# A block-sparse attention with a gated feed-forward behind it: fused scores, wider turns, six chunks for the dense rows, and another plan

## The chip, the cores and the metric

One Trainium2 chip; the kernel is one launch on one of its cores. The time is device time in microseconds (us), as the median of several runs. A core has five engines with queues of their own: TensorE (PE, matmuls, results into eight PSUM banks), VectorE (DVE), ScalarE (ACT), GpSimd (POOL) and SyncE (SP, which here issues DMA transfers). 16 DMA engines move the data.

## The reference

Four batches, eight heads, 768 tokens in 24 blocks of 32, head size 64. Each query block sees its own block and its neighbours, the first and the last block, and three sampled blocks; the first and the last query block see everything. The attention's output goes through a gated feed-forward (512 to 1536 to 512).

```python
scores = np.matmul(q, k.transpose(0, 1, 3, 2)) / np.sqrt(D)
mask = np.abs(blk_i - blk_j) <= 1
mask = mask | (blk_i == 0) | (blk_j == 0) | (blk_i == n_blocks - 1) | (blk_j == n_blocks - 1)
for qb in range(n_blocks):
    for kb in sampled_blocks[qb]:
        mask[qb*32:(qb+1)*32, kb*32:(kb+1)*32] = True
attn = softmax(np.where(mask, scores, -1e9))
x = np.matmul(attn, v)            # (4, 8, 768, 64) -> (3072, 512)
out = (sigmoid(x @ w_gate) * (x @ w_val)) @ w_out
```

## The kernel before, in words

The function builds a list of operations first. Each one has an engine (or a choice of two), a planned duration, the operations it depends on, a priority, and the buffers it takes and releases. A planner (`Planner.run`) then simulates the engines and picks, again and again, the operation that can start first, the lower priority number among those that can start at nearly the same time. The order that comes out is written into the queues of the engines and fixed. A wait at run time therefore holds up everything behind it on the same engine. `switch` is the planned price of a change of PE between full-size matmuls and matmuls on 64x64 or 64x32 tiles of the array; transfers are planned with one rate for SP and one for POOL.

**Load (L375, POOL's queue).** For each batch K, V and Q are loaded with a cast to 16 bits into four staging buffers `stg` of 96 partitions, eight tokens per partition. In batch 0 the order is K, V, Q. The weights (L390, L398) follow in chunks, which the list `GATES` holds back until certain gathers have been issued.

**Turn (L484, L492, L497, L499).** K and Q are transposed on PE, per pair of heads in 16 transposes of 96x64 (two heads side by side, as 64-column tiles of the array), and evacuated by DVE or ACT into `KT` and `QT`. Tokens in `KT` stand in the order (j, p): token 8p+j lies at column 96j+p.

**V's road (L526, L534, L546, L563, L569, L627).** DVE regroups V by rows; four transfers write it to the DRAM buffer `scr`; from there SP gathers, for each query block, the three neighbours (L563, several blocks at once, into `V1`) and the three sampled blocks (L627, three transfers of 32 KB, into `V2`). The block numbers stand in registers of SP (L413). POOL copies the first and the last block into the remaining 32 rows (L569).

**A step** is two query blocks with all eight heads; a batch has 11. POOL copies the sampled keys into one of four buffers `KG` (L605, three copies per block, and L614 for the first and last block). PE computes masks and scores as 64x32 tiles (L648, L655) into two PSUM banks. DVE takes the maximum in each bank (L666), ACT the exponentials with their sums (L677), DVE the reciprocal (L684) and the scaling (L696; the planner may put it on ACT in its plan, but the instruction written is DVE's). PE transposes the probabilities (L708), DVE or ACT evacuates them (L714), PE multiplies with V (L733), and the result goes to `XA` (L749, L754).

**Dense rows.** For the first and the last query block, per pair of heads: scores over 768 keys in two banks (L774), two maxima and their combination (L784, L785), two exponentials (L792), sum, reciprocal and scaling (L801 to L803), eight transposes of 96 columns (L813), evacuation (L818), eight products (L831), result to `XA` (L848). There are 4 such pieces per batch.

**Feed-forward.** Nine groups of 128, 128, 256, 256, 256, 512, 512, 512 and 512 tokens. For each of 12 chunks of the hidden size: gate and value matmuls (L884, four each), tanh on ACT (L892), product on DVE (L897); then 12 matmuls per 128 tokens (L915), scaling (L922, L924), store (L929). Its evacuations have the first priority in the plan.

**PSUM banks.** Scores use banks 0 to 2 (two for each step), transposes and products 2 and 3, the feed-forward 4 to 7 (the last two groups all eight).

Of the kernel before, what the change touches and what calls it, by code (L numbers as in the profile page):

```python
# [26 lines left out]
NEG = -1.0e30  # L27

# [19 lines left out]

class Planner:
# [10 lines left out]
    def __init__(self):  # L60
        self.ops = []
        self.held = {}

# [5 lines left out]
    def run(self, switch=0.12, dma_lat=1.8):  # L69
        free = {e: 0.0 for e in self.ENG}  # L70
        slot_free = {}
        slot_held = {}
        handles = {}
        dma_free = {e: 0.0 for e in self.ENG}
        lanes = {e: [0.0] * self.LANES for e in self.ENG}
        mode = 128
        for o in self.ops:
            o.outs = []
            o.nwait = len(o.deps) + len(o.after)
            o.ready = []  # L80
# [11 lines left out]
        n = len(self.ops)  # L92
        while len(order) < n:
            best = None
            for e in self.ENG:
                ests = []
                for o in cand[e]:
                    t = free[e]
                    for tr, er, lat in o.ready:
                        t = max(t, tr + (lat if er != e else 0.0))  # L100
                    if o.dma:
                        t = max(t, lanes[e][min(o.ndma, 3) - 1])
                    ok = True
                    got = {}
                    for h, slots in o.acq:
                        c = [(slot_free.get(s, 0.0), k, s) for k, s in enumerate(slots)
                             if s not in slot_held and s not in got.values()]
                        if not c:
                            ok = False
                            break  # L110
                        now = [x for x in c if x[0] <= t]
                        x = min(now, key=lambda x: x[1]) if now else min(c)
                        got[h] = x[2]
                        t = max(t, x[0])
                    if ok:
                        if e == "PE" and o.mode != mode:
                            t += switch
                        ests.append((t, o, got))
                if not ests:
                    continue  # L120
                lo = min(x[0] for x in ests)
                pick = min((x for x in ests if x[0] <= lo + (0.12 if e == "PE" else 0.02)),
# [20 lines left out]
            o.eng, o.dur = e, o.durs[o.engs.index(e)]  # L143
            if e == "PE":
# [6 lines left out]
            if o.dma:  # L151

                share = 3.0 if e == "SP" and dma_free["POOL"] > o.end else 1.0
                dma_free[e] = max(dma_free[e], o.end) + o.dma * share
                if e == "SP":
                    dma_free["POOL"] += o.dma
                o.end = dma_free[e] + dma_lat
                lanes[e] = lanes[e][o.ndma :] + [o.end] * o.ndma
# [4 lines left out]
            for h in o.rel:  # L163
# [3 lines left out]
                slot_free[s] = o.end + o.lat  # L167
            for x in o.engs:
                cand[x].remove(o)
            for w, whole in o.outs:  # L170
                w.nwait -= 1
                w.ready.append((o.end, e, o.lat) if whole else (o.start + o.dur, e, 0.0))
# [9 lines left out]
def kernel(  # L182
# [45 lines left out]
    banks = [psum.tile([128, 512], f32, tag=f"bank{i}", name=f"bank{i}") for i in range(8)]  # L228
# [14 lines left out]

    KT = [sb(f"KT{r}", [128, NP, S]) for r in range(2)]
    QT = [sb(f"QT{r}", [128, NP, S]) for r in range(2)]
    KT4 = [t.rearrange("d a (j p) -> d a j p", p=TP) for t in KT]

    KW4 = [t.bitcast(f32).rearrange("d a (j p) -> d a j p", p=TP // 2) for t in KT]
    stg = [sb(f"stg{r}", [TP, H * TJ * D]) for r in range(4)]
    stages = [("stg", r) for r in range(4)]  # L250
    by_head = lambda t: t.rearrange("p (h j d) -> p h j d", h=H, j=TJ)
    by_row = lambda t: t.rearrange("p (j h d) -> p j h d", h=H, j=TJ)
# [14 lines left out]
    DP = [sb(f"DP{s}", [128, TJ, 128]) for s in range(2)]  # L267
    DPT = [sb(f"DPT{s}", [128, TJ, 128]) for s in range(2)]
# [41 lines left out]
    GATES = {7: 2, 9: 4, 10: 6, 11: 8}  # L310
    WCH, WOH = 4, 3

    TURN_DMA = 4
    VGATHER = [("SP", 1.6)] * 4

    K_DMA, KQ_SP = 4, 3.0
    SC_DUR = 0.36
# [14 lines left out]
    def f_memset(o):  # L332
        pin(nc.gpsimd.memset(ones, 1.0))
        pin(nc.gpsimd.memset(mrow, 0.0))
        for d in DP:
            pin(nc.gpsimd.memset(d.rearrange("q j p -> q (j p)").bitcast(f32), 0.0))

    def f_mask(o):
# [5 lines left out]
        pin(V.tensor_scalar(kidx[:, 0 : NB * 3], in0=sbv.rearrange("p a o -> p (a o)"), scalar1=2, scalar2=None, op0=ALU.mult))  # L344
# [16 lines left out]
    o_ms = P("memset", "POOL", 1.4, f_memset, prio=-40)  # L361
# [5 lines left out]
    def load(name, src, b, prio, after=(), parts=1):  # L367
# [4 lines left out]
        for x in range(parts):  # L372
            def f(o, x=x):
                t = by_head(stg[pl.handles[h][1]])[:, x * n : x * n + n]
                pin(nc.gpsimd.dma_start(t, src[b, x * n : x * n + n].rearrange("h (p j) d -> p h j d", j=TJ)))  # L375

            res.append(P(f"ld{name}{b}{x}", "POOL", 0.8, f, after=list(after) + res[-1:], prio=prio,
                         acq=[(h, stages)] if x == 0 else [], dma=3.9 / parts))
# [28 lines left out]
    def f_regs(eng, key, part):  # L407
        def f(o):
            e = {"SP": nc.sync, "POOL": nc.gpsimd}[eng]
            et = {"SP": mybir.EngineType.SP, "POOL": mybir.EngineType.Pool}[eng]  # L410
            src, unit = (kidx, 2) if eng == "POOL" else (vidx, BLK)
# [26 lines left out]
    pgb = bk(4, 5, 6, 7)  # L438
    spool = bk(0, 1, 2)
    early = bk(0, 1, 4, 5, 6)  # L440
    ptpool = bk(2, 3)
    xpool = bk(3, 2)
# [13 lines left out]
    def attention(b, prio0, ldeps):  # L456
# [5 lines left out]
        if b == 0:  # L462
            ldk, hk = load("k", k, b, pp - 0.050, ldeps, np_)
            ldv, hv = load("v", v, b, pp - 0.049, ldk[-1:])
            ldq, hq = load("q", q, b, pp - 0.048, ldv[-1:], np_)
# [8 lines left out]
        for nm, ld, hs, res, TT in (("k", ldk, hk, kops, KT[r]), ("q", ldq, hq, qops, QT[r])):  # L474
            if nm == "q" or b < K_DMA:
                for p in range(NP):
                    h = f"tr{nm}{b}{p}"

                    def f_tr(o, hs=hs, p=p, h=h):
                        t = by_head(stg[pl.handles[hs][1]])  # L480
                        ps = banks[o.slots[h][1]].bitcast(f16)[:, 0:S].rearrange("d (j p) -> d j p", p=TP)
                        for j in range(TJ):
                            for hh in range(2):
                                pin(nc.tensor.transpose(ps[64 * hh : 64 * hh + 64, j, :], t[:, 2 * p + hh, j, :], ident[0:TP, 0:TP]))  # L484

                    tr = P(f"tr{nm}{b}{p}", "PE", 0.47, f_tr, deps=[ld[p * np_ // NP], c_dma] + kq_users[b - 2], prio=pp - 0.040,
                           acq=[(h, early if b == 0 else xpool)], mode=64, rel=[hs] if p == NP - 1 else [])

                    def f_ev(o, nm=nm, p=p, h=h, TT=TT):
                        ps = banks[o.slots[h][1]].bitcast(f16)[:, 0:S]  # L490
                        if nm == "k":
                            pin(copy(o)(TT[:, p, :], ps))  # L492
                            return
                        ps = ps.rearrange("d (j b c) -> d b j c", b=NB, c=4)
                        dst = TT[:, p, :].rearrange("d (b j c) -> d b j c", b=NB, c=4)
# [5 lines left out]
                    res.append(P(f"ev{nm}{b}{p}", ("DVE", "ACT"), (0.48, 0.7), f_ev, deps=[tr], prio=pp - 0.040, rel=[h]))  # L501
            else:

                hsh = f"sh{nm}{b}"

                def f_sh(o, hs=hs, hsh=hsh):
                    t = by_head(stg[pl.handles[hs][1]])
                    d = stg[o.slots[hsh][1]].rearrange("p (a j e d) -> p a j e d", a=NP, j=TJ, e=2)
                    for hh in range(2):
                        pin(nc.vector.tensor_copy(d[:, :, :, hh, :], t[:, hh : H : 2]))  # L510

                shs.append(P(f"sh{nm}{b}", "DVE", 1.3, f_sh, deps=ld, prio=pp - 0.045, rel=[hs], acq=[(hsh, stages)]))

                ldq[0].after.append(shs[0])

                def f_tt(o, hsh=hsh, TT=TT):
                    pin(nc.sync.dma_start(TT.rearrange("d a (j p) -> d (a j) p", p=TP), stg[o.slots[hsh][1]], transpose=True))

                res.append(P(f"tt{nm}{b}", "SP", KQ_SP, f_tt, deps=shs[-1:] + kq_users[b - 2], prio=pp - 0.040, rel=[hsh], dma=3.5))
# [4 lines left out]
        def f_vsh(o):  # L524
            t = by_head(stg[pl.handles[hv][1]])
            pin(nc.vector.tensor_copy(by_row(stg[o.slots[f"vr{b}"][1]]), t.rearrange("p h j d -> p j h d")))  # L526

        vs = P(f"vsh{b}", "DVE", 1.14, f_vsh, deps=ldv, prio=pp - 0.045, rel=[hv],
               acq=[(f"vr{b}", stages)])

        def f_scr(o):
            dst = scr[b].rearrange("(b j c) n -> c b j n", j=TJ, c=4)
            for c in range(4):
                pin(nc.sync.dma_start(dst[c], vrows(o).rearrange("(b c) (j n) -> c b j n", c=4, j=TJ)[c]))  # L534

        sc = P(f"scr{b}", "SP", 3.2, f_scr, deps=[vs], prio=pp - 0.045, dma=2.2, ndma=3)
        scr_ops.append(sc)
        if b == 0:
            FF["gate"][0].after.append(sc)
# [5 lines left out]
        def f_fl(o):  # L545
            pin(nc.sync.dma_start(FL[96:128, 0, :], scr[b][0:BLK, :]))  # L546
            pin(nc.sync.dma_start(FL[96:128, 1, :], scr[b][S - BLK : S, :]))

        fl = P(f"vfl{b}", "SP", 1.0, f_fl, deps=[sc] + fl_users[b - 1], prio=bp - 1.55, dma=0.2, ndma=2)
# [6 lines left out]
        for (i0, n), x in zip(wins, turn):  # L556
# [3 lines left out]
            def f_w(o, i0=i0, n=n, x=x):  # L560
                src = scr[b][(i0 - 1) * BLK : (i0 - 1) * BLK + 96, :]
                src = bass.AP(tensor=src.tensor, offset=src.offset, ap=[[DM, 96], [BLK * DM, n], [1, DM]])
                pin(nc.sync.dma_start(V1[x][0:96, 0:n, :], src))  # L563
# [411 lines left out]
```

## Time and profile before

| | us |
|---|---|
| median of 3 runs (lowest to highest) | 355.77 (355.77 to 358.47) |
| the profiled execution | 354.82 |
| its span, first to last instruction | 353.0 |
| busy in the span: PE, DVE, ACT, POOL | 315.2, 245.2, 211.3, 107.7 |
| last product of the attention (L733) starts | 294.5 |
| DMA: bytes moved, share of 16 engines (SP's and POOL's queue) | 42.05 MB, 27.1% and 25.8% |

Matmuls are pipelined and their ends are modelled, so PE's busy time is an upper bound of the work in it. Lines of groups read: line, engine, operation, output<-input, count, busy us, mean ns, idle time before and who ended it. Lines of the chain and of the timeline begin with the start and the duration in us.

### The profile page before, as it was taken

Reading aid. Unit: us, or ns where it says so; the run is one execution under the profiler, and the core shown is the slowest. Engines: PE = TensorE matmul, PEld = TensorE weight load, DVE = VectorE, ACT = ScalarE, POOL = GpSimd, SP = SyncE. Lnnn points to the kernel's source line nnn. Section 1 sums busy time; section 2 is a strip of 40 time slices with the busy share of each in tenths; the row PEclk is TensorE's granted clock in tenths of the full one; section 3 lists DMA queues with packets and bytes.
Section 4 is the critical chain, followed back from the end, with each engine's and each line's share of the span. In section 5 each row is a group of like instructions: output and inputs, shape, how many; then the busy total and the mean of one; then the engine's idle time right before and its main releaser. Section 6 shows DMA issues by size and latency. Waiting matters only on the chain.

```text
span 353.0 us, 13181 instructions
## 1 busy us (share of the span) xinstructions
PE 315.2 (89%) x4864; PEld 202.8 (57%) x4864; DVE 245.2 (69%) x647; ACT 211.3 (60%) x688; POOL 107.7 (31%) x361
## 2 busy tenths in 40 slices
PE   2557988999797979989999999999999999999995
PEld 1336776667573667667856655555555555444442
DVE  1586889788698785789977999597789594303320
ACT  2265677675494776688866868657765574223321
POOL 5449853016248141354501246331021200000000
PEclk9999989999899998999999999999999999999999
DMA  7996999999943879232343243334313210020002
GB/s 121 195 188 149 190 223 231 223 209 234 231 118 111 167 137 196 79 101 77 113 142 104 83 110 99 116 109 113 84 45 95 87 45 0 2 83 36 3 30 89
DMA packets 44132, 42.05 MB, mean 119 GB/s; under 512 B 5923, under 2 KB 40996, under 8 KB 44068
## 3 DMA queue, kind: packets, MB, share of 16 engines
q1 hardware_dynamic: 28820, 27.06, 27.1%
q0 software_dynamic: 15248, 14.16, 25.8%
q8 instruction: 38, 0.62, 0.7%
q14 instruction: 26, 0.21, 0.2%
HBM read 45.91 MB, written 9.44 MB: 157 GB/s over the span
## 4 chain that ended last, share of the span: by engine, by line
PE 57%; DMA 16%; DVE 11%; ACT 7%; SPq 4%; issue 3%; POOL 0%; ACTq 0%; DVEq 0%; POOLq 0%
PE bank L884 27%; PE bank L915 14%; DMA V<-scr 11%; PE bank L733 4%; ACT P L677 4%; PE bank L708 4%; DVE P L696 3%; DMA stg<-in_v_dram 3%; DVE NM L666 2%; DMA out_dram<-YS 2%; PE bank L655 2%; SPq L627 2%; DVE HT L897 2%; PE bank L648 1%; PE bank L813 1%
## 5 line engine op out<-in xcount | busy, mean ns | idle before, releaser
L677 ACT ACTIVATE P<-bank,NM 128x256 f16<-128x256 f32 x176 | 81.6, 476 | 26.0 <-DVE NM L666 24.8
L605 POOL COPY KG<-KT 128x64 f32 x264 | 51.3, 243 | 112.1 <-PE bank L655 104.4
L884 PE MATMUL bank<-XA,wv 128*128 128x512 f16 (+2 forms) x432 | 82.4, 315 | 1.0 <-DMA wv<-in_moe_w_val_dram 0.6
L884 PE MATMUL bank<-XA,wg 128*128 128x512 f16 (+2 forms) x432 | 82.5, 315 | 0.9 <-ACT TH L892 0.4
L897 DVE SCALAR_TENSOR_TENSOR HT<-TH,bank 128x512 f16<-128x512 f32 (+2 forms) x108 | 54.3, 505 | 39.0 <-PE bank L884 36.6
L892 ACT ACTIVATE TH<-bank 128x512 f32<-128x512 f32 (+2 forms) x108 | 48.9, 458 | 37.7 <-PE bank L884 32.7
L915 PE MATMUL bank<-wo,HT 128*128 128x512 f16 x288 | 65.2, 379 | 2.6 <-DVE HT L897 2.6
L666 DVE TENSOR_REDUCE NM<-bank 128x2 f32<-128x512 f32 x88 | 57.4, 682 | 5.9 <-PE bank L655 5.7
L884 PEld LDWEIGHTS <-wv 128*128 128x128 f16 x432 | 38.8, 101 | 25.4 <-issue 2.2
L884 PEld LDWEIGHTS <-wg 128*128 128x128 f16 x432 | 37.2, 101 | 21.7 <-issue 2.6
L915 PEld LDWEIGHTS <-HT 128*128 128x128 f16 x288 | 27.2, 98 | 34.6 <-issue 3.9
L696 DVE TENSOR_SCALAR P<-P,ZZ 128x256 f16<-128x256 f16 x176 | 45.8, 320 | 1.5
L569 POOL COPY V<-FL 32x1024 f32<-32x1024 f32 (+1 forms) x32 | 30.1, 978 | 23.7 <-PE bank L733 16.8
L733 PE MATMUL bank<-PTS,V 128*128 128x64 f16 x704 | 30.7, 196 | 6.5 <-DMA V<-scr 6.1
L677 ACT ACTIVATION_READ_ACCUMULATOR P<-bank,NM 128x1 f32 x176 | 36.4, 207 | 0.0
L733 PEld LDWEIGHTS <-V 128*128 128x128 f16 x704 | 27.6, 100 | 14.3 <-issue 4.6
L708 PE MATMUL bank<-ident,P 128*128 128x128 f16 x352 | 29.1, 227 | 5.4 <-ACT DP L792 1.2
L749 ACT CAST XA<-bank 64x256 f16<-64x256 f32 x62 | 22.6, 364 | 15.3 <-PE bank L733 13.2
L708 PEld LDWEIGHTS <-P 128*128 128x128 f16 x352 | 23.5, 102 | 11.0 <-issue 5.6
L714 DVE COPY PTS<-bank 128x1024 f16<-128x1024 f16 x37 | 25.3, 683 | 5.7 <-PE bank L708 5.0
L484 PE MATMUL bank<-ident,stg 96*64 96x96 f16 x512 | 18.3, 228 | 11.9 <-DMA stg<-in_k_dram 6.1
L924 ACT ACTIVATE YS<-bank 128x512 f32<-128x512 f32 x22 | 13.1, 598 | 24.1 <-PE bank L915 21.1
(61 smaller groups left out, 307.0 us busy)
## 6 DMA issues: line engine op xcount, KB each, us to landing
V<-scr SPq DMA_DIRECT2D x264, 32.0 KB
out_dram<-YS SPq DMA_DIRECT2D x24, 256.0 KB
V<-scr SPq DMA_DIRECT2D x16, 288.0 KB
stg<-in_v_dram POOLq DMA_DIRECT2D x4, 768.0 KB, 10.2
scr<-stg SPq DMA_DIRECT2D x16, 192.0 KB
V<-scr SPq DMA_DIRECT2D x8, 384.0 KB
stg<-in_k_dram POOLq DMA_DIRECT2D x3, 768.0 KB, 12.4
stg<-in_q_dram POOLq DMA_DIRECT2D x3, 768.0 KB, 13.1
```

The lines of the kernel that those rows point to most:

```text
L569: pin(nc.gpsimd.tensor_copy(vt[x][96:128, 0:n, :].bitcast(f32), FL[96:128, c : c + 1, :].bitcast(f32).broadcast_to([BLK, n, DM // 2])))
L605: pin(nc.gpsimd.tensor_copy(t[:, :, 1 + n], KW4[r][:, :, :, bass.ds(vals[(i % 8) * 3 + n], 2)]))
L666: pin(nc.vector.tensor_reduce(NM[pl.handles[hz][1]][:, 2 * hh : 2 * hh + 2], t, axis=AX.X, op=ALU.max, negate=True))
L677: pin(nc.scalar.activation(pb[:, u, :], t[:, u, :], AF.Exp, bias=NM[z][:, x : x + 1], scale=1.0, accum_out=ZZ[z][:, x : x + 1]))
L696: pin(nc.vector.tensor_scalar(pb[:, u, :], in0=pb[:, u, :], scalar1=ZZ[z][:, 2 * hh + u : 2 * hh + u + 1], scalar2=None, op0=ALU.mult))
L708: pin(nc.tensor.transpose(t[:, c * 128 : c * 128 + 128], pb[:, c * 128 : c * 128 + 128], ident))
L714: pin(copy(o)(PTS[pl.handles[hTS][1]].rearrange("k c q -> k (c q)"), banks[o.slots[hT][1]].bitcast(f16)))
L733: pin(nc.tensor.matmul(t[:, u, p, :], vt[:, ws, p * 128 : p * 128 + 128], pt[:, u, c, :, 32 * p : 32 * p + 32], start=(c == 0), stop=(c == ...
L884: pin(nc.tensor.matmul(t, wt[:, c, f_ * 128 : f_ * 128 + 128], XT[g][:, c, :], start=(c == 0), stop=(c == 3)))
L892: pin(nc.scalar.activation(TH[o.slots[ht][1]][:, 0:n], banks[o.slots[hg][1]][:, 0:n], AF.Tanh, bias=0.0, scale=0.5))
L897: pin(nc.vector.scalar_tensor_tensor(HT[:, f_, hoff : hoff + n], in0=TH[o.slots[ht][1]][:, 0:n], scalar=1.0, in1=banks[o.slots[hv][1]][:, ...
L915: pin(nc.tensor.matmul(t, HT[:, f_, hoff + tt * 128 : hoff + tt * 128 + 128], wo[:, f_, :], start=(f_ == 0), stop=(f_ == NF - 1)))
```

## The change

It has these parts:

1. **Planner.** Transfers of both queues are simulated together (`Transfers`), with lower rates while both queues have work; the price of a mode change is 0.16 instead of 0.12; PE waits up to 1 us (`WAIT`) before it leaves full-size matmuls for a lone small-tile operation; a table `OFFSETS` shifts the priority of each kind of operation in each batch; in planned gaps of PE between 7 and 60 us, dummy matmuls on the identity are put in (`fill`).
2. **Banks.** Pairs of banks are one tile. Scores take pair (0,1) or (2,3), transposes and products bank 4 or 3, the feed-forward banks 5 to 7 (the last two groups all eight).
3. **Fused scores.** In batches 2 and 3 the scores of steps 0 and 1, 2 and 3, and so on, and of the dense pieces 0 and 1, 2 and 3, are one operation of PE. One DVE instruction takes the maxima of both banks of a step.
4. **Head pairs.** In batches 1 to 3, POOL or DVE regroups K and Q by rows first; PE then transposes the 128 columns of a head pair at once, 8 transposes of full width per piece instead of 16. `KT` now holds the tokens in order.
5. **Dense rows.** 6 chunks of 128 keys instead of 8 of 96; one maximum and one exponential instruction over both banks.
6. **V.** It is loaded first in batch 0, as 128 partitions of six tokens, and written to `scr` by one transfer; in batch 0 SP or ACT may issue that transfer, the first window and the two edge blocks. Q of batch 0 is loaded and turned in two parts by tokens (64 and 32 of the 96 partitions). There are five staging buffers.
7. **Order of loads.** Weights wait for gathers of blocks 4, 7, 9, 10 and 11; the loads of the next batch wait for the gather of block 12 (batch 0) or 10.
8. **Scaling.** Where the planner picks ACT for L696's work, ACT now does it. The copies of edge blocks may go to DVE.

```diff
-    def run(self, switch=0.12, dma_lat=1.8):
+    def run(self, switch=0.16):
...
+                if e == "PE" and mode == 128:
+                    full = [x for x in ests if x[1].mode == 128]
+                    part = [x for x in ests if x[1].mode != 128 and x[0] <= free[e] + switch + 0.05]
+                    if full and min(x[0] for x in full) <= free[e] + 0.05 and len(part) == 1 and free[e] < self.since.setdefault(id(part[0][1]), free[e]) + WAIT:
+                        ests = full
...
+    twin = [psum.tile([128, 1024], f32, tag=f"bank{i}", name=f"bank{i}") for i in range(4)]
+    banks = [twin[i // 2][:, 512 * (i % 2) : 512 * (i % 2) + 512] for i in range(8)]
...
-    GATES = {7: 2, 9: 4, 10: 6, 11: 8}
+    GATES = {0: 4, 2: 7, 4: 9, 6: 10, 8: 11}
+    LGATE = {1: 12, 2: 10, 3: 10}
+    PAIRS = ["d0 d1", "d2 d3", "s0 s1", "s2 s3", "s4 s5", "s6 s7", "s8 s9"]
+    TOGETHER = [[], [], PAIRS, PAIRS]
...
-    pgb = bk(4, 5, 6, 7)
-    spool = bk(0, 1, 2)
-    early = bk(0, 1, 4, 5, 6)
-    ptpool = bk(2, 3)
-    xpool = bk(3, 2)
+    pgb = bk(5, 6, 7)
+    spool = [tuple(bk(x, x + 1)) for x in (0, 2)]
+    spool0 = [tuple(bk(x, x + 1)) for x in (0, 2, 6)]
+    early = bk(0, 1, 2, 5, 6)
+    ptpool = bk(4, 3)
+    xpool = bk(4, 3)
+
+    def scores(b, unit, name, dur, fn, deps, prio, acq, rel=()):
+        both = next((x for x in TOGETHER[b] if unit in x.split()), unit)
+        if (b, both) not in made:
+            fns = [fn]
+            def f(o):
+                for x in fns:
+                    x(o)
+            made[b, both] = P(name, "PE", dur, f, deps=deps, prio=prio, mode=32, acq=acq, rel=rel), fns
+            return made[b, both][0]
+        o, fns = made[b, both]
+        fns.append(fn)
+        o.deps += deps
+        o.acq += acq
+        o.rel += rel
+        o.durs = (o.durs[0] + dur,)
+        return o
...
-            ldk, hk = load("k", k, b, pp - 0.050, ldeps, np_)
-            ldv, hv = load("v", v, b, pp - 0.049, ldk[-1:])
-            ldq, hq = load("q", q, b, pp - 0.048, ldv[-1:], np_)
+            ldv, hv = load("v", v, b, pp - 0.050, ldeps)
+            ldk, hk = load("k", k, b, pp - 0.049, ldv[-1:], np_)
+            ldq, hq = load("q", q, b, pp - 0.048, ldk[-1:], np_, tokens=True)
...
+                def f_sh(o, hs=hs, hsh=hsh):
+                    t, d = by_head(stg[pl.handles[hs][1]]), by_row(stg[o.slots[hsh][1]])
+                    if o.eng == "POOL":
+                        pin(nc.gpsimd.tensor_copy(d.bitcast(f32), t.bitcast(f32).rearrange("p h j d -> p j h d")))
+                    else:
+                        pin(nc.vector.tensor_copy(d, t.rearrange("p h j d -> p j h d")))
...
+                                pin(nc.tensor.transpose(ps[:, j, :], t[z, j * DM + p * 128 : j * DM + p * 128 + 128], ident[z, z]))
...
+                            pin(copy(o)(TT[:, p, :].rearrange("d (p j) -> d p j", j=TJ), ps.rearrange("d (j p) -> d p j", j=TJ)))
...
-            for c in range(4):
-                pin(nc.sync.dma_start(dst[c], vrows(o).rearrange("(b c) (j n) -> c b j n", c=4, j=TJ)[c]))
+            pin(queue(o).dma_start(scr[b].rearrange("(p j) n -> p (j n)", j=VJ), vrows(o)[:, 0 : VJ * DM]))
...
+            def f_mx(o, hS=hS, hz=hz):
+                t = twin[pl.handles[hS[0]][1] // 2].rearrange("p (x n) -> p x n", n=256)
+                pin(nc.vector.tensor_reduce(NM[o.slots[hz][1]][:, 0:4], t, axis=AX.X, op=ALU.max, negate=True))
...
+                    if o.eng == "ACT":
+                        for u in range(2):
+                            pin(nc.scalar.activation(pb[:, u, :], pb[:, u, :], AF.Copy, scale=ZZ[z][:, 2 * hh + u : 2 * hh + u + 1]))
+                        return
...
+            def f_dmx(o, h0=h0, hz=hz):
+                pin(nc.vector.tensor_reduce(NM[o.slots[hz][1]][:, 0:1], all_keys(h0), axis=AX.XY, op=ALU.max, negate=True))
...
+                pin(nc.scalar.activation(DP[o.slots[hDP][1]].rearrange("p (x n) -> p x n", x=2), all_keys(h0), AF.Exp,
+                                         bias=NM[z][:, 0:1], scale=1.0, accum_out=ZZ[z][:, 0:1]))
...
+                for j in range(VJ):
+                    pin(nc.tensor.transpose(t[:, j * 128 : j * 128 + 128], DP[o.slots[hDP][1]][:, j : S : VJ], ident))
...
+    def fill(t0, t1, mode, held, freed):
+        t0 = max(t0, 7.0)
+        n = int((t1 - t0 - 0.2) / FILL_DUR)
+        if n < 4 or t0 > FILL_END:
+            return None
...
+            for x in range(n):
+                pin(nc.tensor.matmul(banks[y[1]][:, 0:128], ident, ident, start=True, stop=True, skip_group_check=True))
...
+    for o in pl.ops:
+        o.prio += OFFSETS.get(kind(o), 0.0)
```

## The prediction

> **What bounds the kernel now.** I began with the busy time by stage: us of the stage, then busy us of each engine, the clock that TensorE (PE) was granted and the DMA share.
>
> ```profile
> 0.00:20.00 20.00, 8.40 (x221) 6.80 (x224) 7.99 (x27) 5.52 (x9) 11.37 (x38) 1.00 0.91 160
> 20.00:60.00 40.00, 30.93 (x616) 25.26 (x609) 32.87 (x97) 25.98 (x102) 25.81 (x72) 0.96 1.08 195
> 60.00:180.00 120.00, 108.02 (x2066) 80.25 (x2066) 98.80 (x273) 83.93 (x280) 44.04 (x148) 0.97 0.72 153
> 180.00:300.00 120.00, 119.41 (x1751) 68.82 (x1747) 93.82 (x235) 81.52 (x275) 26.52 (x104) 1.00 0.30 88
> 300.00:353.00 53.00, 48.43 (x224) 21.69 (x222) 11.70 (x17) 14.33 (x24) 0.00 (x0) 0.99 0.10 40
> ```
>
> From 180 us on PE has no gap (119.41 of 120): there, PE work removed is time removed, and relief for the other engines is worth nothing. Before 180 us it has gaps. Second view, the chain of waits over the first 60 us:
>
> ```profile
> 2.76 9.44 DMA stg<-in_v_dram
> 12.32 1.24 DVE stg L526
> ...
> 17.11 3.08 DMA scr<-stg
> ...
> 21.18 8.31 DMA V<-scr
> ...
> 35.65 6.48 DMA V<-scr
> 42.15 5.36 DMA V<-scr
> ```
>
> That is the road of V: loaded third (behind K), regrouped, written to DRAM by four transfers (issued 13.57 to 17.89), gathered back. The gathers set the end of this stage. Third, the costliest groups, for durations:
>
> ```profile
> L666 DVE TENSOR_REDUCE NM<-bank 128x2 f32<-128x512 f32 x88 | 57.4, 682 | 5.9 <-PE bank L655 5.7
> L696 DVE TENSOR_SCALAR P<-P,ZZ 128x256 f16<-128x256 f16 x176 | 45.8, 320 | 1.5
> L784 DVE TENSOR_REDUCE NM<-bank 128x1 f32<-128x384 f32 x32 | 16.2, 548 | 0.1
> L526 DVE COPY stg<-stg 96x4096 f16<-96x4096 f16 x4 | 5.2, 1295 | 1.6 <-DMA stg<-in_v_dram 1.4 <-issue 0.2
> ```
>
> Busy PE is not PE at its pitch, so I counted the matmuls of 60 to 180 us and multiplied by the undisturbed pitches of the timeline: 512 columns 0.216 us (96 in 20.72 at the end of the chain), eight 128-column transposes 0.45, sixteen of L733 0.47, one step's scores 0.50 and 0.10 for entering the 32-row mode. That gives about 98 us, so 22 of the 120 are lost. The waits name one part: L733 on V gathers 4.9 us; and the clock falls to 0.50 for 3.41 us from 92.4 and from 133.4, each just after such a wait, 1.7 us lost each time. DMA is thus behind 8.3; the other 13.7 belong to evacuations on DVE and ScalarE (ACT) and to waits between groups.
>
> **PE work removed.** (a) Dense rows: in 16 pieces, 8 transposes and 8 products become 6 and 6: 64 matmuls at 0.056 = 3.6 us. (b) K and Q of batches 1 to 3: 24 pieces, now 16 half transposes in 0.46 us plus some 0.09 to enter the 64-row mode (four 256-wide matmuls take 0.44, but 0.53 when this piece follows); then 8 full ones, 0.36 to 0.45 by the pitch of L708's, with no mode. Gain 0.09 to 0.19 each; some pieces already follow each other, so I take 0.12, 2.9 us (2.2 to 4.6). (c) Fused scores: 7 of 15 pieces go in batches 2 and 3, 14 mode entries at 0.10 = 1.4 us (0 to 2.8). Sum 7.9 us (5.8 to 11.0), on the path where PE is full; where it has gaps it only counts if the next wait moves too, and that is the next term.
>
> A fused piece waits for the copied keys of four units, the whole ring of four buffers, and for banks 0 to 3. Behind it in PE's queue stand feed-forward matmuls. Refilling the ring takes 12 copies of L605 at 0.243 = 2.9 us on POOL, after the piece that frees it. From 180 to 300 us 18 steps ran, 6.7 us each, so 13 us per pair: covered, at no cost. Without that cover each of 14 pieces would pay up to 2.9.
>
> **DVE and ACT.** The two reduce rows give 134 ns for 128 columns, so one reduce over 1024 takes 1.22 against 2 x 0.682: 0.15 x 44 = 6.4 us less DVE. Dense: 0.95 against 2 x 0.548 + 0.249, and the 0.18 sum goes: 9 us less. ACT's dense exponentials: 2 x (0.58 + 0.20) become one of about 1.09, 7.5 us less. All 176 scalings of L696 run on DVE now, those the planner gave to ACT too; in the new code ACT really runs its share. Against this, six regroupings of K and Q (1.3 us by L526; on POOL twice L569's 0.98 for half the data), K's evacuation with a strided read (0.55 now, at most doubled, 16 times). DVE is relieved by 10 to 30 of its 245 us. None of it counts from 180 us on. Of the 13.7 us above I take a third back, 4.5 (0 to 9). The regrouping delays each load's use by 1.2 to 2; batch 1's loads were issued from 52.1 and first turned at 74.1, so they arrive early; uncovered it would be 3 x 2.
>
> A POOL regrouping holds DVE up, too: L696 averages 0.39 us for the 56 that overlap a POOL copy and 0.29 for the others. At most six times 2 us, kept for the range; I count nothing, because DVE has slack against PE in every stage. The Trainium skill (GPSIMD Engine Reference, section Specifications) says that POOL shares its SBUF interfaces with VectorE and contends with its two-port modes. That speaks against putting these copies on POOL, and this trace agrees (0.39 against 0.29); by it alone the sum would lose up to these 12 us.
>
> **Start.** V is now loaded first. The first half of K landed at 6.1 and the second at 8.4, so V lands near 8 rather than 12.2; one transfer (0.5 issue, 3.1 landing, up to 5 beside K and Q) puts it into DRAM near 13.5 rather than 20.2. K comes as much later, but Q completes the same three loads at 16.5 as before, and first scores stay near 17. So the gathers start 6.7 earlier, and products wait for the probabilities' transposes (24.7). Bytes to move are the same; the queue of gathers and weights starts earlier. I take 5 us (0 to 9). The first weights now wait for a V gather's issue, with POOL's key copies behind them in its queue; today they are issued at 18.02, land 7.4 later and are first used at 37.9, 12 us of cover. V's load becomes 1024 packets instead of 768 (95 ns each over 16 engines by the queue rows: 1.5 us more), its way to DRAM 128 instead of 768 (53 ns each: 2.1 less); they cancel. Issuing some of batch 0's transfers from ACT costs ACT 0.4 us each while it idles.
>
> Weights, loads and gathers are reordered by a model in which gathers crawl while POOL loads run. Of the 8.3 us of DMA waits and slow clock I take 5 (0 to 7).
>
> **Dummy matmuls** fill planned PE gaps up to 60 us. In this trace 32 transposes took 1.49 us up to 17 us and 0.87 at 98.5, and the pitch halves at 41.2: the early PE runs at half rate. Half of 22 us of work could shrink, but PE idles 18 of those 40 us, so I take 1 (from -1, dummies ahead of late work, to 4). The Trainium skill (TensorE: Matmul & The Clock Gate, section What's actually happening) has the clock halved by default and after an idle window of about 3.4 us; the lengths of 3.41 agree, though here waits of 2.3 and 2.6 us were enough. By it, with the fill, all of the early half rate would go, about 4 instead of 1.
>
> **Sum**: 7.9 + 4.5 + 5 + 5 + 1 = 23.4. The profiled execution took 354.82 (span 353.0 and 1.8 around it): 331.4; the median of the runs lies 0.95 above that execution, so **332 us**. Bounds: all lower ends save 4.8, all upper ends 40.
>
> **Rivals.** One: transfers bind the start anyway and the chip does not follow the plan's rates; only PE work goes: 355.8 - 7.9 = 348 (345 to 351). For it: DMA share 1.08 to 1.25 from 40 to 90 us, same bytes. Against: only 0.91 before. Chance 0.17. Two: the plan holds everywhere, three quarters to all of the upper ends: 316 to 324. For it: PE idles 11.6 + 9.1 + 12.0 us before 180. Against: every term would have to come out at its best. 0.12. Three, slower: the feed-forward keeps **three banks instead of four**. A gate bank is held for its matmuls, 0.2 to the release and ACT's tanh, a value bank likewise with DVE's product: at 256 columns 0.44 + 0.2 + 0.38 and 0.44 + 0.2 + 0.41, together 2.07 of the 3 x 0.88 bank-us of a chunk; so each evacuation may be late by 0.28 us, at 512 columns (0.86, 0.60, 0.69) by 0.89. Four banks allowed 0.7 and 1.7. A product queued behind a 1.22 us reduce then stops PE 0.94 us (0.33 at 512). With 36 chunks of 256 columns and 24 of 512 that is at most 42 us; it cancels the gain when more than 56% of them meet it. At 70% it is 29: 361 (359 to 373). Against: evacuations have the planner's first priority, and PE has attention work between chunks. 0.11. Within 1%, a mixture: 0.05. The rest, 0.55, is the forecast (324 to 342).
>
> Faster by over 1% (about what a measurement here can tell from no change): 0.55 + 0.17 + 0.12 = 0.84; same 0.05; slower 0.11. The range 316 to 354 leaves out the slower rival and little else.
>
> **What would show it.** Profile after: transposes and products of the dense rows 96 each; reduce about 1.2 us, 44 times; the first V gather near 14 and first products near 25; PE busy share in 60 to 180 above 0.93 and fewer half-clock windows; attention's last product before 280 instead of 294.6. Wrong if PE waits on HT (L897) or TH (L892) at the feed-forward grow past 10 us, if V waits stay at 6, or if PE has new gaps after 180.

## The result, and the profile after

The changed kernel takes **411.50 us** (median of 4 runs, 409.21 to 413.28), the kernel before 355.77 (4 runs, 355.37 to 358.47). The ratio is 1.154 (1.146 to 1.163): 56 us slower, where 332 us were forecast. The profiled execution has a span of 411.5 us.

The same table by stage as before the change: us of the stage, busy us of PE, its weight loads, DVE, ACT and POOL, granted clock, DMA share, GB/s.

```profile
0.00:20.00 20.00, 12.75 (x195) 11.98 (x197) 6.90 (x26) 2.88 (x3) 6.58 (x24) 0.76 0.95 179
20.00:60.00 40.00, 29.87 (x746) 26.14 (x743) 29.64 (x70) 26.07 (x92) 23.45 (x65) 0.82 0.99 171
60.00:180.00 120.00, 96.77 (x1717) 71.89 (x1715) 84.38 (x202) 77.65 (x247) 35.08 (x116) 0.99 0.59 130
180.00:300.00 120.00, 96.48 (x1409) 56.22 (x1407) 78.06 (x163) 73.33 (x226) 23.02 (x97) 1.00 0.41 97
300.00:411.00 111.00, 91.90 (x807) 46.33 (x805) 45.02 (x101) 45.77 (x122) 4.01 (x22) 0.98 0.12 40
```

PE was full from 180 to 300 us before (119.41 of 120); now it has gaps there, 23.5 us, and 23.2 us from 60 to 180 (12.0 before). DVE and ACT are less busy than before in both stages and DMA is far from full (0.59 and 0.41), so none of them is the new bound. PE, DVE and ACT all wait, which points to waits on each other. The waits of PE in the profile after, longest sum first (line waited for: us in total, times, longest):

```profile
PE bank L1031 <- DVE HT L1044: 7.6, 14, 0.9
PE bank L1031 <- ACT TH L1039: 4.6, 10, 0.6
PE bank L1031 <- DVE PTS L875: 4.2, 6, 1.4
PE bank L1062 <- ACT XA L904: 3.9, 6, 0.9
PE bank L1031 <- ACT PTS L875: 3.7, 5, 0.9
```

L1031 are the feed-forward's gate and value matmuls (L884 before), L1062 its output matmuls (L915). The first two rows are the feed-forward's own evacuations, product and tanh: 12.2 us, above the 10 that the prediction named as a sign of error. The next three are stranger. `PTS` is attention's probabilities, evacuated from bank 4 or 3; `XA` is attention's result, from the same banks. Feed-forward matmuls, which write banks 5 to 7, have no business with either. Before the change the waits of PE show no such pair, and L884 waited 1.0 us for its own two evacuations. One piece of the timeline shows how this looks (start, duration, instruction, idle time before and who ended it):

```profile
190.76 0.70 PE L888 MATMUL bank<-PTS,V 128*128 128x64 f16 x16 [0.21 <-ACT PTS L875]
191.30 2.75 PE L1062 MATMUL bank<-wo,HT 128*128 128x512 f16 x12
194.09 0.74 ACT L904 CAST XA<-bank 64x256 f16<-64x256 f32 x2 [3.38 <-PE bank L1062]
194.88 0.61 PE L869 MATMUL bank<-ident,P 128*128 128x128 f16 x8 [0.83 <-ACT XA L904]
```

Here attention's products (L888) go into bank 4 and the feed-forward's output (L1062) into bank 5. ACT could evacuate bank 4 once the products end, near 191.5. It starts at 194.09, when the twelve matmuls into **bank 5** have ended. And the transposes (L869), which need bank 4 again, stop PE for 0.83 us. Banks 4 and 5 are the two halves of one tile now.

The costliest groups that the prediction priced:

```profile
L823 DVE TENSOR_REDUCE NM<-bank 128x4 f32<-128x1024 f32 x44 | 52.8, 1217 | 4.6 <-PE bank L814 4.4
L939 DVE TENSOR_REDUCE NM<-bank 128x1 f32<-128x768 f32 x16 | 14.9, 949 | 1.9 <-PE bank L929 1.9
L963 PE MATMUL bank<-ident,DP 128*128 128x128 f16 x96 | 8.2, 225 | 3.5 <-ACT DP L945 1.3 <-DVE DP L954 1.1 <-DVE HT L1044 1.0
L976 PE MATMUL bank<-DPT,stg 128*128 128x128 f16 x96 | 7.8, 219 | 3.2 <-DVE DPT L968 1.9 <-DVE HT L1044 0.8 <-ACT TH L1039 0.4
```

These durations came out as forecast (1.217 against 1.22; 0.949 against 0.95; 96 and 96). The price of single operations was not the problem.

### The profile page after: what moved, and what is told of

The parts are those of the page before. It is cut to its first block, busy times and chain, and to the rows that moved or that the text cites. A ratio compares the mean times of both kernels' runs of the same rounds, so it can differ in the third digit from the quotient of the medians.

```text
span 411.5 us, 12938 instructions
## 1 busy us (share of the span) xinstructions
PE 327.8 (80%) x4858; PEld 212.6 (52%) x4858; DVE 244.0 (59%) x557; ACT 225.7 (55%) x685; POOL 92.1 (22%) x322
## 3 DMA queue, kind: packets, MB, share of 16 engines
q1 hardware_dynamic: 25892, 26.20, 22.4%
## 5 line engine op out<-in xcount | busy, mean ns | idle before, releaser
L1031 PE MATMUL bank<-XA,wv 128*128 128x512 f16 (+2 forms) x432 | 80.6, 309 | 19.8 <-DVE HT L1044 4.2
L1031 PE MATMUL bank<-XA,wg 128*128 128x512 f16 (+2 forms) x432 | 80.7, 309 | 17.1 <-ACT TH L1039 3.5
L1062 PE MATMUL bank<-wo,HT 128*128 128x512 f16 x288 | 68.2, 390 | 7.4 <-ACT XA L904 3.9
L1031 PEld LDWEIGHTS <-wv 128*128 128x128 f16 x432 | 38.6, 98 | 47.0 <-issue 26.5
L1031 PEld LDWEIGHTS <-wg 128*128 128x128 f16 x432 | 37.9, 98 | 41.0 <-issue 20.6
L823 DVE TENSOR_REDUCE NM<-bank 128x4 f32<-128x1024 f32 x44 | 52.8, 1217 | 4.6 <-PE bank L814 4.4
L1062 PEld LDWEIGHTS <-HT 128*128 128x128 f16 x288 | 28.3, 100 | 40.0 <-issue 11.9
L858 DVE TENSOR_SCALAR P<-P,ZZ 128x256 f16<-128x256 f16 x150 | 34.9, 289 | 1.3
L888 PE MATMUL bank<-PTS,V 128*128 128x64 f16 x704 | 29.1, 194 | 7.2 <-DVE HT L1044 3.4
L888 PEld LDWEIGHTS <-V 128*128 128x128 f16 x704 | 26.4, 98 | 14.9 <-issue 7.1
L869 PE MATMUL bank<-ident,P 128*128 128x128 f16 x352 | 27.2, 219 | 6.7 <-DVE P L858 3.2
L1071 ACT ACTIVATE YS<-bank 128x512 f32<-128x512 f32 x16 | 9.6, 600 | 38.5 <-PE bank L1062 13.4
L869 PEld LDWEIGHTS <-P 128*128 128x128 f16 x352 | 22.2, 97 | 13.8 <-issue 7.3
L875 DVE COPY PTS<-bank 128x1024 f16<-128x1024 f16 x29 | 19.8, 685 | 10.3 <-PE bank L869 4.6
L1096 PE MATMUL bank<-ident 128*128 128x128 f16 x186 | 17.5, 273 | 5.0 <-DMA ident<-bb_ident 3.2
L875 ACT COPY PTS<-bank 128x1024 f16<-128x1024 f16 x15 | 15.2, 1012 | 8.9 <-PE bank L1062 5.4
```

What stands on the lines that cost most here:

```text
L823: pin(nc.vector.tensor_reduce(NM[o.slots[hz][1]][:, 0:4], t, axis=AX.X, op=ALU.max, negate=True))
L858: pin(nc.vector.tensor_scalar(pb[:, u, :], in0=pb[:, u, :], scalar1=ZZ[z][:, 2 * hh + u : 2 * hh + u + 1], scalar2=None, op0=ALU.mult))
L869: pin(nc.tensor.transpose(t[:, c * 128 : c * 128 + 128], pb[:, c * 128 : c * 128 + 128], ident))
L875: pin(copy(o)(PTS[pl.handles[hTS][1]].rearrange("k c q -> k (c q)"), banks[o.slots[hT][1]].bitcast(f16)))
L888: pin(nc.tensor.matmul(t[:, u, p, :], vt[:, ws, p * 128 : p * 128 + 128], pt[:, u, c, :, 32 * p : 32 * p + 32], start=(c == 0), stop=(c == ...
L1031: pin(nc.tensor.matmul(t, wt[:, c, f_ * 128 : f_ * 128 + 128], XT[g][:, c, :], start=(c == 0), stop=(c == 3)))
```

## Experiments

The kernel before took 354.1 to 354.4 us on the chips of these runs. Each ratio is to it, with a 95% interval. Kernels that change priorities, pools or operations are planned anew; where the planned order of the variant is the same as that of the kernel it was made from, this is said.

### Are shared tiles the cause?

Theory A: two banks in one tile make every user of one bank wait for the users of the other. Rivals: three feed-forward banks are too few (B), the new order is bad on the chip (C), or the dummy matmuls harm.

**Banks 4 to 7 as one tile each** (the first run), banks 0 to 3 still two pairs; the planned order and the banks' places are those of the changed kernel. Where the scores stood in banks 6 and 7 (batch 0), the maximum is taken in two instructions.

```diff
-    twin = [psum.tile([128, 1024], f32, tag=f"bank{i}", name=f"bank{i}") for i in range(4)]
-    banks = [twin[i // 2][:, 512 * (i % 2) : 512 * (i % 2) + 512] for i in range(8)]
+    twin = [psum.tile([128, 1024], f32, tag=f"twin{i}", name=f"twin{i}") for i in range(2)]
+    banks = [twin[i // 2][:, 512 * (i % 2) : 512 * (i % 2) + 512] for i in range(4)]
+    banks += [psum.tile([128, 512], f32, tag=f"bank{i}", name=f"bank{i}") for i in range(4, 8)]
```

> The changed kernel with banks 4 to 7 as a tile each again; banks 0 to 3 stay two pairs (scores); where a step of batch 0 takes banks 6 and 7 the maximum is two instructions. The planned order is the same. Theory A (a pair of banks that is one tile makes the users of its two halves wait for each other): in the last group the changed kernel needs 6.66 us for three chunks of 24 matmuls that last 5.18, 0.49 us lost per chunk, and there are 108 chunks, so some 53 of the 56 us go, and something of the forecast gain shows: 335 to 360. Rival B (three feed-forward banks are too few): at least 400. Rival C (the new order itself is bad on the chip): 385 or more.

Measured: **350.05 us** (347.43 to 351.65), ratio 0.989 (0.980 to 0.997). 61 us are gone by the allocation alone. (The two medians are of different chips, on which the kernel before takes 355.77 and 354.37 us; by the two ratios it is 59 us.) In its table by stage PE is nearly full again from 180 to 300 us:

```profile
60.00:180.00 120.00, 107.81 (x1885) 81.32 (x1883) 98.01 (x227) 90.83 (x294) 36.65 (x124) 0.99 0.70 151
180.00:300.00 120.00, 117.50 (x1698) 67.78 (x1696) 94.28 (x200) 85.42 (x265) 23.95 (x103) 1.00 0.35 92
```

Of PE's waits on the feed-forward's evacuations 4.5 us are left of 12.2 (waits of PE in the same kernel):

```profile
PE bank L1038 <- DVE HT L1051: 3.6, 5, 1.8
...
PE bank L1038 <- ACT TH L1046: 0.9, 3, 0.4
```

The end of the two kernels is the cleanest comparison, because attention is over and only three banks turn. In the changed kernel's timeline:

```profile
372.97 1.02 PE L1031 MATMUL bank<-XA,wv 128*128 128x512 f16 x4 [0.55 <-DVE HT L1044]
...
373.83 1.03 PE L1031 MATMUL bank<-XA,wg 128*128 128x512 f16 x4
...
374.69 1.03 PE L1031 MATMUL bank<-XA,wv 128*128 128x512 f16 x4
374.96 0.69 DVE L1044 SCALAR_TENSOR_TENSOR HT<-TH,bank 128x512 f16<-128x512 f32 x1 [2.05 <-PE bank L1031]
...
375.69 0.60 ACT L1039 ACTIVATE TH<-bank 128x512 f32<-128x512 f32 x1 [2.08 <-DVE HT L1044]
...
376.34 1.02 PE L1031 MATMUL bank<-XA,wg 128*128 128x512 f16 x4 [0.61 <-ACT TH L1039]
...
379.63 1.02 PE L1031 MATMUL bank<-XA,wv 128*128 128x512 f16 x4 [0.55 <-DVE HT L1044]
```

The planned banks of the last group go 6, 7, 5, 6, 7, 5. Every third group of four matmuls waits, and it is always the one into bank 6. What it waits for is the last reader of bank 7 (the product or the tanh just ahead), not that of bank 6, which is one reader older. The readers wait too: the product at 374.96 reads bank 6, whose four matmuls ended near 374.0, but it starts when those into bank 7 end; and the tanh at 375.69, which reads bank 7, starts when that product has ended. Three chunks take 6.66 us (372.97 to 379.63) for 24 matmuls of 0.216 us, 5.18. In the chain of the kernel with banks of their own, the same 96 matmuls in the same order run without a gap:

```profile
311.03 20.73 PE bank L1038 x96
```

**The kernel before, with its eight banks declared as four pairs**, and nothing else; same order.

```diff
-    banks = [psum.tile([128, 512], f32, tag=f"bank{i}", name=f"bank{i}") for i in range(8)]
+    twin = [psum.tile([128, 1024], f32, tag=f"bank{i}", name=f"bank{i}") for i in range(4)]
+    banks = [twin[i // 2][:, 512 * (i % 2) : 512 * (i % 2) + 512] for i in range(8)]
```

> The kernel before with its eight banks allocated as four pairs, nothing else. Theory A: 390 to 420, because its feed-forward uses neighbouring banks one after the other too, and the last 96 gate and value matmuls take 26 to 29 us instead of 20.7. Rivals B and C: 356, unchanged.

Measured: **446.44 us** (442.73 to 450.16), ratio 1.253 (1.244 to 1.262). Pairing alone costs the old kernel 92 us, more than expected; the last 96 gate and value matmuls take 26.6 us (402.37 to 428.92), as expected. Its scores and its transposes share the pair (2,3), and its feed-forward runs across (4,5) and (6,7). PE's waits name both:

```profile
PE bank L885 <- DVE HT L898: 16.6, 26, 1.3
PE bank L649 <- ACT P L678: 13.8, 13, 2.5
PE bank L709 <- DVE NM L667: 7.6, 7, 1.6
```

The last row is transposes (L709, banks 2 and 3) behind the maxima over scores (L667). In this kernel the same banks are used in the same planned order by the same instructions as in the kernel before, so it isn't the use of the memory that makes them wait; it is the waits that the program carries when two banks are one tile.

**Only the pair (4,5) taken apart**, (6,7) left together; same order as the changed kernel.

```diff
+    twin = [None if i == 2 else psum.tile([128, 1024], f32, tag=f"twin{i}", name=f"twin{i}") for i in range(4)]
+    banks = [psum.tile([128, 512], f32, tag=f"bank{i}", name=f"bank{i}") if i in (4, 5)
+             else twin[i // 2][:, 512 * (i % 2) : 512 * (i % 2) + 512] for i in range(8)]
```

> The changed kernel with only banks 4 and 5 as tiles of their own; 6 and 7, both the feed-forward's, stay one tile. It splits the cost of the pairs. Theory A says that waits of the feed-forward for the attention's evacuations in bank 4 and waits inside the pair 6 and 7 both count. In the last group, where the attention is over, 0.49 us are lost per chunk by the pairs of all eight banks; if the pair 6 and 7 carries that alone, 385 to 405; if the pair 4 and 5 carries most, 350 to 370.

Measured: **362.07 us** (360.90 to 363.11), ratio 1.019 (1.012 to 1.027). Of the 61 us, 49 (411.50 to 362.07) hang on the pair that ties attention's transposes and products to the feed-forward, and 12 (362.07 to 350.05) on the feed-forward's own pair, where three chunks of the last group still take 6.66 us (322.80 to 329.46). The split holds for this order of taking the pairs apart; (6,7) alone was not tried. The runs are of different chips, so each difference is good to 1 or 2 us.

### The other parts

**Without dummy matmuls** (the third run), banks 4 to 7 still single; the order of all five engines is that of the first run.

```diff
-    pl.fill = fill
+    pl.fill = None
```

> As the first run, and without the dummy matmuls. If these hold real work back (54 of them run from 27.2 to 32.0 us in the changed kernel while scores stand behind them), this is 3 to 6 us faster than the first run; if they help by the clock, it is up to 4 us slower; if neither matters, equal.

Measured: **345.48 us** (344.44 to 349.19), ratio 0.979 (0.971 to 0.987). With dummies the kernel takes 4.6 us more by the medians, where a gain of 1 was forecast; the ranges of the two overlap (347.43 to 351.65 with them). The dummies do what they are for. In the timeline of the kernel with dummies (first fence) eight transposes take 0.62 us at 31 us; without (second) 1.01 at 32.6:

```profile
26.40 4.37 PE L1103 MATMUL bank<-ident 128*128 128x128 f16 x54
30.70 0.28 PE L808 MATMUL twin<-mrow,ones 64*32 64x192 bf16 x8
...
31.21 0.62 PE L876 MATMUL bank<-ident,P 128*128 128x128 f16 x8
...
42.79 0.39 PE L1038 MATMUL bank<-XA,wg 128*128 128x128 f16 x4
```

```profile
27.46 0.36 PE L808 MATMUL twin<-mrow,ones 64*32 64x192 bf16 x8 [3.34 <-ACT P L842]
...
32.64 1.01 PE L876 MATMUL bank<-ident,P 128*128 128x128 f16 x8 [0.78 <-ACT PTS L882]
...
42.81 0.63 PE L1038 MATMUL bank<-XA,wg 128*128 128x128 f16 x4
```

The Trainium skill (TensorE: Matmul & The Clock Gate, section What's actually happening) would have the early half rate go with steady work; the two lines agree on that, 0.62 against 1.01.

But 54 dummies stand in PE's queue from 26.40 for 4.37 us: the next scores start at 30.70, without dummies at 27.46. This delay does not by itself explain the loss, though. Both kernels run the same matmuls in the same order, and at 42.8 us they stand at the same place (the last line of each fence). At the last dummies (53 us) the kernel with dummies is 2.4 us late, at 75 us 0.3. Some 4 us come up between 97 and 207 us, where neither kernel has a dummy. Why is not known, so the expectation's 3 to 6 us came true without its reason being shown.

**Without the table of offsets**, dummies in.

```diff
-        o.prio += OFFSETS.get(kind(o), 0.0)
+        o.prio += 0.0
```

> As the first run, and with the table of priority shifts all zero, so the planner writes another order. If the table is what makes the plan good, 5 to 25 us slower than the first run; if it fits the plan to durations that the chip does not have (rival C), equal or faster.

Measured: 352.22 us (350.01 to 355.99), ratio 0.993 (0.989 to 0.997), 2.2 us slower than with it, a difference inside the spread of the runs. The table is worth a few us at most.

**K loaded first again** (the K-first run), then V and Q; no dummies.

```diff
-            ldv, hv = load("v", v, b, pp - 0.050, ldeps)
-            ldk, hk = load("k", k, b, pp - 0.049, ldv[-1:], np_)
+            ldk, hk = load("k", k, b, pp - 0.050, ldeps, np_)
+            ldv, hv = load("v", v, b, pp - 0.049, ldk[-1:])
...
```

> The third run (own banks for the feed-forward, no dummies; 345.5 us) with batch 0 loaded in the order K, V, Q as in the kernel before. In the third run V's way to DRAM took from 9.8 to 17.7 us beside the loads of K and Q, K's first transposes came at 10.9 instead of 6.1, and at 60 us PE had done 23.1 us of work against 26.0 before. Theory (loading V first costs the start what it should have gained): 2 to 5 us faster, 340.5 to 343.5. Rival (V first gains as forecast and something else makes the start late): 3 to 6 us slower.

Measured: **344.74 us** (343.44 to 345.23), ratio 0.972 (0.965 to 0.979), the fastest of all; 0.7 us from the third run on another chip, and the intervals of the ratios overlap: no difference can be told. The start does improve. Counting the matmuls done by 60 us times their undisturbed pitches, V first is some 3 us of work behind the kernel before, K first some 1. (The levels depend on the pitches taken for small matmuls: with those of the prediction the kernel before has done some 22 us, not the expectation's 26; the difference holds.) The 2 us are given back by 300 us, where the order behind differs too. So V first gained nothing at the start; it lost. One reason is seen here: with K first, V's one transfer to DRAM is issued at 14.44 instead of 9.95, but takes 3.9 us instead of 7.9, so the first gather starts at 18.36, only 0.5 us later than in the third run (17.86), while K is turned first at 6.43 instead of 10.89.

**Scores not fused** (no dummies, V first).

```diff
-    TOGETHER = [[], [], PAIRS, PAIRS]
+    TOGETHER = [[], [], [], []]
```

> The third run without the fused scores: each step and each dense piece of batches 2 and 3 is an operation of its own. By the price of 14 mode entries at 0.10 us: 1.4 us slower. Rival (a fused piece takes all four score banks and the whole ring of key buffers, and so holds others up): 2 to 6 us faster. In both cases another order comes out of the planner, worth a few us either way.

Measured: 355.46 us (353.22 to 358.08), ratio 1.004 (0.999 to 1.008), 10 us slower than with fusing. Only 11 more entries into the 32-row mode were counted, 1.1 us at 0.10. Between 120 and 240 us PE's gaps grow by 5.6 us, under an order that was planned anew with an offset table fitted to the fused order. This run doesn't separate the two, and what fusing alone is worth stays open.

**K and Q turned in half pieces everywhere**, no regrouping by rows (no dummies, V first).

```diff
+TURN128 = False
...
-            if b:
+            if TURN128 and b:
...
```

> The third run with K and Q of batches 1 to 3 turned in half pieces as before, without the regrouping copies. By the PE work: 24 pieces at 0.12 us, 2.9 us slower (2.2 to 4.6). Rival (six copies of 1.3 to 2 us on DVE or POOL and the delay of the loads cost more than the turns save): up to 5 us faster.

Measured: 350.53 us (348.86 to 352.88), ratio 0.990 (0.986 to 0.995), 5.0 us slower than the third run, though on another chip and under an order planned anew. As the run before shows what a new order can cost, 5.0 is not the price of the turns alone.

**A fourth feed-forward bank** (bank 4 shared with attention; K first, no dummies).

```diff
-    pgb = bk(5, 6, 7)
+    pgb = bk(5, 6, 7, 4)
```

> The K-first run (own banks 4 to 7, no dummies, order K, V, Q; 344.7 us) with bank 4 offered to the feed-forward as a fourth bank, after 5, 6 and 7; it stays offered to transposes and products too, and the planner writes another order. The rival of three banks, as priced in the prediction, gives back up to 42 us by stops behind a reduce; by the waits of the third run (PE on the feed-forward's evacuations 4.2 us in all) it can give at most 4. If three banks hurt: 3 to 10 us faster. If they do not: within 3 us, or slower, since the attention loses its bank at times.

Measured: 349.40 us (347.75 to 352.73), ratio 0.991 (0.986 to 0.995). Slower by 4.7 us, not faster. That alone could be the attention's loss of its bank, or the new order. But PE's waits of the gate and value matmuls for their evacuations are only 4.5 us in the K-first run and 2.9 here: a fourth bank had little to give, and three were not short.

**All scalings on DVE** (K first, no dummies).

```diff
-    SCALE_ENG, SCALE_DUR = ("DVE", "ACT"), (0.49, 0.85)
+    SCALE_ENG, SCALE_DUR = "DVE", 0.58
```

> The K-first run with all scalings (176 instructions) planned and done on DVE, none on ACT; the order is planned anew. Theory (DVE's relief is worth a few us before 180 us): DVE gets some 30 x 0.29 = 8 us of work back, ACT loses 30 x 0.45 = 13; 1 to 5 us slower. Rival (ACT holds up as much as DVE frees): equal or up to 3 faster.

Measured: 347.90 us (345.03 to 348.54), ratio 0.984 (0.976 to 0.992). That is 3.2 us slower: ACT's share of the scalings, 30 of 176 in the K-first run (26 in the changed kernel), and the new order together.

**Every bank its own tile**, so each two-bank instruction becomes two (K first, no dummies, same order as its parent).

```diff
-                if y >= 4:
+                if True:
                     for hh in range(2):
                         t = banks[y + hh].rearrange("p (x n) -> p x n", n=256)
...
-                pin(nc.vector.tensor_reduce(NM[o.slots[hz][1]][:, 0:1], all_keys(h0), axis=AX.XY, op=ALU.max, negate=True))
+                for n, h in enumerate((h0, h1)):
+                    pin(nc.vector.tensor_reduce(z[:, n : n + 1], banks[pl.handles[h][1]][:, 0:384], axis=AX.X, op=ALU.max, negate=True))
...
```

> The K-first run with every bank a tile of its own and each instruction over two banks as two (step maxima, dense maxima with their combination, dense exponentials with their sum); planned durations and so the order stay as they are. DVE gets 44 x 0.15 + 16 x 0.58 = 16 us of work more, ACT 16 x 0.47 = 7.5. If the one-piece instructions are worth their share of the 4.5 us that the prediction took: 1 to 6 us slower. If the pairs left in the scores' banks still make false waits: faster, by up to 4.

Measured: 348.69 us (347.70 to 350.47), ratio 0.988 (0.982 to 0.995). The one-piece instructions on banks 0 to 3 are worth 3.9 us, net of any false waits left in those pairs. That is all that pairing brought, against the 61 us that it cost on banks 4 to 7.

## Why the prediction was wrong

**The step that failed** is one without a number. The list of the change says that pairs of banks are one tile, and the prediction priced what follows from it as an instruction (one reduce, one exponential) but not as a wait. The two lines of the allocation add waits to evacuations and to the first matmuls into a bank, with feed-forward matmuls queued behind them on PE, and these waits were costed at nothing. Measured on the changed kernel: 61 us. The prediction's own sign came true, PE gaps after 180 us and feed-forward waits above 10, and pointed at the right lines.

Two things there could have been read beforehand. In the diff, `ptpool` and `xpool` use bank 4 while `pgb` starts at 5, so attention and feed-forward share a tile. And from 180 us on PE had 0.6 us of slack in 120: a kernel in that state can't take any new wait for nothing.

**Rival Three** (slower, 361) had the right direction and place, the feed-forward's banks, but the wrong mechanism. A fourth bank took less than 2 us off PE's waits and the kernel became 4.7 us slower. With single banks and no dummies (345.48) PE's waits for the feed-forward's evacuations sum to 4.2 us: three banks feed it.

The other terms are read from the kernel with single banks and no dummies. Its span is 342.6, against 353.0 in the profiled execution before, 10.4 us less (8.9 by the medians of one chip), where the terms without dummies promised 22.4. By matmuls times pitch, its total is 5.3 us smaller, and by stage it gets 2.9 us less done up to 60 us, 5.5 more from 60 to 180 and 2.4 more from 180 to 300: 5.3 - 2.9 + 5.5 + 2.4 = 10.3. (Each term is good to some 0.5 us, as the pitch of small matmuls can be taken in more than one way.) Attention's last product starts at 297.1, not before 280.

- **PE work removed**, 7.9 forecast: 5.3 in matmuls (this count leaves out mode entries). Entries into the 32-row mode from full-size matmuls fell from 53 to 38, near the 14 that were forecast, 1.5 us at 0.10; they explain part of the 2.4. Fusing has 11 of them, as the kernel without it shows. About right, at the lower end (5.8). Undoing the head pairs cost 5.0, above the 2.2 to 4.6, with the new order in it.
- **DVE and ACT** 4.5, and **DMA** 5: together 5.5 more work in 60 to 180 us instead of 9.5. The relief is real (one-piece instructions 3.9; scaling on ACT 3.2 with its new order). PE's busy share there is 0.92, not above 0.93. PE's waits of the products for V gathers fell from 6.1 us to 3.2, not to nothing, and the spells of half clock between 60 and 180 us from two to one (61.2 to 64.6).
- **Start**, 5 forecast: -2.9, the second wrong step. V landed early, at 8.7. The step that failed is the next: one transfer of 768 KB from ACT's queue, priced at 3.1 to 5 us, was issued at 9.76 in the changed kernel, and SP waited for it until 17.69:

```profile
SPq L719 <- DMA scr<-stg: 13.6, 1, 13.6
```

  So the first gather started at 17.69 instead of the forecast 14, and the first products at 36.2 instead of 25 (34.7 without dummies); before they began at 29.7. K, second in line now, was first turned at 10.70 instead of 6.10. The forecast that first scores stay near 17 failed with it: without dummies Q is turned at 17.84 and 19.75, and the first scores start at 21.57.
- **Dummies**, 1 forecast with a floor of -1 ("dummies ahead of late work"): -4.6 by the medians. The named risk is seen at 26 to 31 us, but PE has made it up by 43 us; the sign came out wrong, and why the time is lost after 97 us stays open.

**Rival One**'s 345 to 351 holds the kernel with single banks, with dummies (350.05) and without (345.48), though not for its reason: parts that it gave nothing did gain, and the start lost. That its number fits is luck.

## What to carry to other kernels

Before two buffers are merged into one tile for the sake of a wider instruction, list every engine that touches either half: each pair of them now waits on each other, and the price is paid where the fullest engine stands between two of these users. Merge only buffers that are filled and drained together (the two score banks of a step: 3.9 us gained), and keep those of independent streams apart (61 us lost). Work put into gaps of a planned order stands ahead of real work in a fixed queue (here 54 dummies held scores up by 3.2 us), so look whether the gap is where the plan has it.

## What the runs showed of the hardware

- The transfer of V into DRAM, 768 KB from ACT's queue, took 7.9 us when it was issued at 9.76 beside the loads of K and Q, and 3.9 us in the K-first run, issued at 14.44 when they were nearly done. Size and queue are the same, so the traffic beside it is what differs: from 8 to 16 us the DMA share is 1.1 to 1.2 with V first, and with K first 0.44 from 16 to 20. Landing V earlier thus moved the first gather by only 0.5 us.
- Early PE work without dummies runs at half its pitch up to the first entry in the trace's clock record: 41.2 us in the kernel before, 44.1 in the third run (eight transposes 1.01 us ahead of it, 0.61 behind). The granted clock reads 1.00 up to there all the same, so the column does not tell the rate ahead of its first entry.
- With dummies the first entry comes sooner, but not in the same place, and full clock does not last: in the changed kernel it is full from 6.8 to 10.2 us and 0.50 from there to 30.7, in the first run, with the same planned order, full from 18.7 with 0.50 from 25.5 to 28.9.
